# Two halves of a group of transposes sent to TensorE together, and two one-column products made one

## The chip, the core and the metric

The kernel runs on one core of a Trainium2 chip. The metric is the device time of one execution in microseconds; the time before is the median of three runs. The engines are named as in the profile: PE (TensorE, with PEld for its weight loads), DVE (VectorE), ACT (ScalarE), POOL (GpSimd) and SP (SyncE). SP and POOL also issue the transfers (DMA).

## The reference

A delta rule runs over 768 tokens for 4 batches of 8 heads of width 48, and two two-layer networks (384 to 2048 to 384) follow on its 3072 token rows.

```python
k_n = k / (np.linalg.norm(k, axis=-1, keepdims=True) + 1e-06)
for t in range(S):
    kt, vt, bt = (k_n[:, :, t], v[:, :, t], beta[:, :, t, None])
    y[:, :, t] = np.einsum('bhd,bhde->bhe', q[:, :, t], state)
    v_old = np.einsum('bhde,bhd->bhe', state, kt)
    state = state + bt[:, :, :, None] * np.einsum('bhd,bhe->bhde', kt, vt - v_old)
...
h = x @ w_in
g = np.maximum(h, 0.0) + alpha * np.minimum(h, 0.0)
x = g @ w_out
...
h = np.maximum(x @ w_in, 0.0)
return h * h @ w_out
```

## The kernel before

The tokens are cut into 12 chunks of 64, and each chunk into two units, one for each half of the batches and heads (unit u = 2c + s). Three kinds of work run side by side.

**Early work**, unit by unit, ahead of the scan (`early`). `keys` scales the keys, splits them into a high and a low half in 16 bits (`kh`), and spreads them (`ktb`). `transp` (L308) turns both halves: for each half, eight products with an identity go into one PSUM bank (L322), and ACT or DVE copies that bank out three times (`kf`, and `kbd` for each of two heads). `gram` (L339) multiplies them (L344), copies the result out (`gs`, in the trace `r` or `pf`) and stores it to DRAM (`gscr`, L348, from SP's queue). When both chunks of a pair are stored, they are loaded as `prob` (L360), and `inverse` solves 31 columns one after the other on DVE (L386, L387). Its result goes through DRAM (`tscr`, L395) into `diag`.

The banks of early work come from `ebank`: for chunks 0 and 1 four banks in turn (`acc0`, `acc1`, `acc2`, `pe`), from chunk 2 on two banks in turn (`pe`, `acc2`). Each bank has one buffer, so the next user waits until the last copy out of it is done.

**The scan**, chunk by chunk (`steps`, `both`): `b_r` (products of `kbd` with the state `shl`), `b_u0` (with `diag`), `b_go` (with `cross`), `b_u1` (with `diag` again), `b_s` (the new state, `ktb`), `b_p` and `b_y` (the output, products with `sbd` and `ubd`, L131). ACT copies the output out (`t<-pa`), SP stores it (`x1d`, L517) and loads it again as `xf` (L544, L545); ACT and DVE split that into `xh` (L558) and `xl` (L559). Before each chunk, `scales` also finds two powers of two: `ranges` (L257) squares and sums the values and queries into the two columns of `tot` (L265, L266, L268), two products with a matrix of ones sum over the partitions (L271, L272), and a few small DVE operations make the factors `sc`.

**The first network** for each chunk: 16 groups of nine products `h` (L617), an activation on ACT and DVE, a split into `gh` (L629) and `gl` (L630), and nine products `acc` (L649). Layer two follows over pairs of chunks. Before the first chunk, 16 tiles of `w1` are loaded by POOL (L586) and split: ACT copies (`sbd` or `t`, L108), four DVE operations, four products (L597, L598), two casts (L601), two products (L602), two casts (L603).

The order on each engine isn't written by hand. Every step has a time on a list of events (`at`, `run_to`), which sets its priority, and a scheduler places instructions engine by engine from priorities, buffers and modelled times. Each engine then runs its own list strictly in order.

Of the kernel before, what the change touches and what calls it, by code (L numbers as in the profile page):

```python
# [22 lines left out]
CH = 64  # L23
# [6 lines left out]
HD = 2 * D  # L30
# [58 lines left out]
def kernel(ctx: ExitStack, tc: tile.TileContext, qT, ktok, vtok, beta, w1, w2, alpha, cmask, hmask, eye, ident, out):  # L89
# [50 lines left out]
    def ebank(c):  # L140

        return next(two if c > 1 else spare)
# [85 lines left out]
    def scales(c):  # L228
        ss = new(erl, [128, 16], F32, "ss", 2)
        if c:  # L230
            kts[c] = new(erl, [128, 16, D], F32, "ktr")
            G.dma_start(out=kts[c], in_=ktok[c])
        kt = kts[c]
        for v in range(2):
            s2 = bank(128, D, ebank(c))
            A.activation(out=s2, in_=kt[:, 8 * v:8 * v + 8], func=ACTF.Square)
            V.tensor_reduce(out=ss[:, 8 * v:8 * v + 8], in_=s2, axis=AX.X, op=ALU.add)
        n = new(erl, [128, 16], F32, "n", 2)
        r = new(erl, [128, 16], F32, "r", 2)
        A.activation(out=n, in_=ss, func=ACTF.Sqrt)  # L240
        V.tensor_scalar(out=r, in0=n, scalar1=1e-30, scalar2=None, op0=ALU.max)
        V.reciprocal(out=r, in_=r)
        V.tensor_tensor(out=r, in0=ss, in1=r, op=ALU.mult)
        V.tensor_tensor(out=n, in0=n, in1=r, op=ALU.add)
        V.tensor_scalar(out=n, in0=n, scalar1=0.03125, scalar2=6.25e-8, op0=ALU.mult, op1=ALU.add)
        nr[c] = new(erl, [128, 16], F32, "rk", 2)
        V.reciprocal(out=nr[c], in_=n)

        def loads():
            for v in range(2):  # L250
                vs[2 * c + v] = new(stp, [128, NG, D], F32, "vr", 2)
                G.dma_start(out=vs[2 * c + v], in_=vtok[c, :, 8 * v:8 * v + 8])
                qs[2 * c + v] = new(stp, [HD, NG, CH], F32, "qr", 2)
                G.dma_start(out=qs[2 * c + v], in_=qT[2 * c + v])

        def ranges():

            sq = new(erl, [128, 2, 2], F32, "sq", 2)
            for v in range(2):
                for i, t in enumerate((vs[2 * c + v], qs[2 * c + v])):  # L260
                    p = t.shape[0]
                    j = psum.tile([128, 512], F32, tag="pe", name="pe", bufs=PB["pe"])[0:p, 0:NG * t.shape[2]]
                    A.activation(out=j, in_=t.rearrange("p g e -> p (g e)"), func=ACTF.Square, accum_out=sq[0:p, i, v:v + 1])
            tot = new(erl, [128, 2], F32, "tot", 2)
            V.tensor_reduce(out=tot[:, 0:1], in_=sq[:, 0:1], axis=AX.X, op=ALU.add)  # L265
            V.tensor_reduce(out=tot[0:HD, 1:2], in_=sq[0:HD, 1:2], axis=AX.X, op=ALU.add)  # L266
            if c:
                V.tensor_tensor(out=tot[:, 0:1], in0=tot[:, 0:1], in1=cum[0][:, 0:1], op=ALU.add)  # L268
            cum[0] = tot
            ps = psum.tile([128, 512], F32, tag="pe", name="pe", bufs=PB["pe"])  # L270
            nc.tensor.matmul(ps[:, 0:1], lhsT=ones, rhs=tot[:, 0:1], start=True, stop=True)  # L271
            nc.tensor.matmul(ps[:, 1:2], lhsT=ones[0:HD], rhs=tot[0:HD, 1:2], start=True, stop=True)  # L272
            t = new(stp, [128, 8], F32, "sc", 3)
            e = t[:, 0:2].bitcast(U32)
            V.tensor_copy(out=t[:, 0:2], in_=ps[:, 0:2])
            V.tensor_scalar(out=e, in0=e, scalar1=24, scalar2=None, op0=ALU.logical_shift_right)
            V.tensor_scalar(out=e, in0=e, scalar1=-1.0, scalar2=200.0, op0=ALU.mult, op1=ALU.add)
            V.tensor_scalar(out=e, in0=e, scalar1=23, scalar2=None, op0=ALU.logical_shift_left)
            V.reciprocal(out=t[:, 2:4], in_=t[:, 0:2])
            V.tensor_tensor(out=t[:, 3:4], in0=t[:, 2:3], in1=t[:, 3:4], op=ALU.mult)  # L280
            V.tensor_scalar(out=t[:, 4:5], in0=t[:, 2:3], scalar1=0.0625, scalar2=None, op0=ALU.mult)
            V.tensor_scalar(out=t[:, 5:6], in0=t[:, 2:3], scalar1=-0.0625, scalar2=None, op0=ALU.mult)
            V.tensor_scalar(out=t[:, 6:7], in0=t[:, 2:3], scalar1=-0.00390625, scalar2=None, op0=ALU.mult)
            sc[c] = {"v": t[:, 0:1], "q": t[:, 1:2], "y": t[:, 3:4], "s": t[:, 4:5], "r": t[:, 5:6], "g": t[:, 6:7]}

        return loads, ranges
# [3 lines left out]
    def early(u):  # L290
# [16 lines left out]
        def transp():  # L307
# [5 lines left out]
            else:  # L313
                whole = new(erl, [HD, 2, NG, 128], F16, "kbdE") if c else new(stp, [HD, 2, NG, 128], F16, "kbd", 2)
                kbd = [whole[:, i] for i in range(2)]
                kf = new(erl, [HD, 2, NG, CH], F16, "kf") if c else new(stp, [HD, 2, NG, CH], F16, "qh", 2)
            d["kbd"] = kbd
            for i in range(2):
                ps = bank(128, CH, ebank(c))
                for g in range(NG):  # L320
                    w = wide(ktb, i, g)
                    nc.tensor.matmul(ps[0:w.shape[1], g], lhsT=w, rhs=i2, start=True, stop=True)  # L322
                ps = ps[0:HD]
                scaled(kf[:, i], ps)
                for h in range(2):
                    o, k = heads(kbd[i])[:, :, :, h], ps.rearrange("p g (b i) -> p g b i", b=2)
# [495 lines left out]
```

## Time and profile before

| what | us |
|---|---|
| median of three runs | 1141.21 (1141.11 to 1142.35) |
| the profiled execution's own time | 1141.8 |
| its span, first to last instruction | 1140.0 |
| PE, DVE, ACT, POOL busy | 1052.6, 735.1, 729.9, 122.2 |
| mean granted TensorE clock | 0.976 of full speed |

The span has three stages. The opening lasts until the first product `h` of chunk 0 at 153.3 us; the first network and the scan run together until about 755 us; the second network runs alone after that. A busy time says how long an engine worked, not whether anything waited for it; which wait ended last is read from the chain of waits and from the timelines. In a timeline a row gives the start, the time, the engine and line, the tiles written and read, and in brackets the idle time before it with what ended it.

### The profile page before, as it was taken

The page shows a single profiled execution, that of the slowest core. Times are in us where ns is not written, and L with a number is a line of the kernel's source. Part 1 is how long each engine was busy: PE and PEld are TensorE (multiplying, and loading weights), DVE is VectorE, ACT ScalarE, POOL GpSimd, SP SyncE. Part 2 cuts the span into 40 slices and gives each one's busy share as a digit, 9 for nine tenths or more (in the row PEclk, how much of TensorE's full clock was granted, in tenths as well). Part 3 has the DMA queues.
Part 4 walks back from the last instruction along what each step waited for, and adds up shares of the span by engine and source line. Part 5 has one row for each costly group of instructions (what it writes and reads, how often), then busy time and mean ns, then how long its engine had stood idle before and what let it go on. Part 6 is the DMA issues. An engine that isn't in the chain of part 4 may idle for free.

```text
span 1140.0 us, 25239 instructions
## 1 busy us (share of the span) xinstructions
PE 1052.6 (92%) x9952; PEld 934.4 (82%) x9952; DVE 735.1 (64%) x1904; ACT 729.9 (64%) x1583; POOL 122.2 (11%) x214
## 2 busy tenths in 40 slices
PE   2775879899999989998999989999999999999997
PEld 2443579799999988998999989988888888888886
DVE  6969798699889968897996759888312121221211
ACT  7867677867857875885666546577645454554543
POOL 5111111111111111110110001111000000000000
PEclk9887899999999999999999989999999999999999
DMA  9754545744744483555344233343101000010000
GB/s 318 268 138 108 112 134 128 178 127 124 171 109 136 139 176 90 148 146 133 89 110 97 62 112 111 99 137 113 56 1 56 0 28 28 1 56 1 28 1 28
DMA packets 162886, 116.78 MB, mean 102 GB/s; under 512 B 122032, under 2 KB 143536, under 8 KB 162768
## 3 DMA queue, kind: packets, MB, share of 16 engines
q0 software_dynamic: 17472, 73.74, 20.6%
q1 hardware_dynamic: 145296, 41.44, 16.6%
q8 instruction: 78, 1.28, 0.5%
q14 instruction: 40, 0.33, 0.1%
HBM read 75.82 MB, written 39.32 MB: 101 GB/s over the span
## 4 chain that ended last, share of the span: by engine, by line
PE 66%; issue 10%; DMA 7%; ACT 5%; DVE 5%; POOL 1%; SPq 1%; POOLq 0%; DVEq 0%; ACTq 0%
PE h L617 29%; PE acc L649 29%; PE pa L131 4%; PE pa L121 3%; DMA prob<-gscr 2%; DMA gscr<-pf 1%; DMA vr<-in_vtok_dram 1%; DMA xf<-x2d 1%; ACT kbdE L108 1%; SPq L360 1%; ACT r L108 1%; DMA fscr<-kbdE 0%; DVE r L624 0%; DVE gl L630 0%; ACT kf L108 0%
## 5 line engine op out<-in xcount | busy, mean ns | idle before, releaser
L649 PE MATMUL acc<-gh,w 128*128 128x256 f32 (+1 forms) x1728 | 434.2, 323 | 6.6 <-ACT gh L629 5.5
L617 PE MATMUL h<-xh,w 128*128 128x256 f32 (+1 forms) x1728 | 438.4, 324 | 1.2 <-DVE r L624 1.0
L649 PEld LDWEIGHTS acc<-gh,w 128*128 128x128 f32 x1728 | 300.5, 192 | 30.3 <-ACT gh L629 6.1
L630 DVE TENSOR_TENSOR gl<-r,gh 128x256 fp32r<-128x256 f32 (+1 forms) x288 | 145.3, 507 | 277.4 <-ACT gh L629 276.8
L617 PEld LDWEIGHTS h<-xh,w 128*128 128x128 f32 x1728 | 302.8, 191 | 25.1 <-DVE r L624 1.4
L649 PE MATMUL acc<-gl,w 128*128 128x256 f32 (+1 forms) x864 | 276.2, 324 | 2.2 <-DVE gl L630 2.1
L617 PE MATMUL h<-xl,w 128*128 128x256 f32 (+1 forms) x864 | 277.9, 322 | 0.0
L649 PEld LDWEIGHTS acc<-gl,w 128*128 128x128 f32 x864 | 165.8, 192 | 14.8 <-DVE gl L630 3.2
L617 PEld LDWEIGHTS h<-xl,w 128*128 128x128 f32 x864 | 165.7, 192 | 11.3 <-DVE xl L559 0.2
L629 ACT CAST gh<-r 128x256 fp32r<-128x256 f32 (+1 forms) x288 | 136.1, 476 | 49.6 <-DVE r L624 40.0
L626 ACT ACTIVATE r<-h 128x512 f32<-128x512 f32 x96 | 57.1, 596 | 147.9 <-PE h L617 141.0
L108 ACT ACTIVATE r<-h,sgn 128x256 f32<-128x256 f32 x192 | 89.8, 472 | 67.9 <-PE h L617 65.7
L624 DVE SCALAR_TENSOR_TENSOR r<-h,bet,r 128x256 f32<-128x256 f32 x192 | 90.9, 477 | 21.5 <-ACT r L108 20.7
L386 DVE TENSOR_TENSOR col<-prob,inv 128x252 f32<-128x252 f32 (+22 forms) x186 | 63.8, 343 | 1.9
L387 DVE TENSOR_TENSOR inv<-inv,col 128x252 f32<-128x252 f32 (+22 forms) x186 | 63.5, 341 | 1.3
L627 ACT ACTIVATE r<-r 128x512 f32<-128x512 f32 x96 | 60.6, 633 | 2.6
L121 PEld LDWEIGHTS <-kbd 96*128 96x128 f16 x1104 | 37.9, 98 | 11.3 <-issue 8.4
L597 PE MATMUL h<-w,idf 128*128 128x384 f32 x64 | 34.2, 620 | 8.0 <-ACT w L603 7.7
L131 PE MATMUL pa<-ph,ubd 128*128 128x64 f16 (+1 forms) x576 | 39.0, 196 | 0.0
L558 ACT CAST xh<-xf 128x256 fp32r<-128x256 f32 x72 | 25.7, 405 | 17.3 <-DMA xf<-x2d 8.2
L131 PE MATMUL pa<-qh,sbd 96*128 96x64 f16 (+1 forms) x528 | 36.0, 196 | 0.4 <-DVE pf L502 0.4
L559 DVE TENSOR_TENSOR xl<-xf,xh 128x256 fp32r<-128x256 f32 x72 | 26.9, 420 | 13.7 <-ACT xh L558 13.6
(172 smaller groups left out, 1389.2 us busy)
## 6 DMA issues: line engine op xcount, KB each, us to landing
w<-in_w_dram POOLq DMA_DIRECT2D x16, 768.0 KB, 11.9
raw<-in_w_dram POOLq DMA_DIRECT2D x32, 384.0 KB, 3.4
kbd<-fscr POOLq DMA_DIRECT2D x22, 384.0 KB, 4.2
ktb<-kscr POOLq DMA_DIRECT2D x22, 384.0 KB, 3.7
kscr<-ktbE POOLq DMA_DIRECT2D x21, 384.0 KB, 3.5
fscr<-kbdE POOLq DMA_DIRECT2D x21, 384.0 KB, 3.7
vr<-in_vtok_dram POOLq DMA_DIRECT2D x24, 192.0 KB, 3.8
qr<-in_qT_dram POOLq DMA_DIRECT2D x24, 192.0 KB, 3.6
```

The lines of the kernel that those rows point to most:

```text
L108: A.activation(out=out, in_=in_, func=ACTF.Copy if isinstance(scale, float) else ACTF.Identity, scale=scale)
L121: nc.tensor.matmul(ps, lhsT=w[:, i], rhs=x[:, j], start=start and n == 0, stop=stop and n == 2)
L131: nc.tensor.matmul(ps[0:w.shape[1], g], lhsT=w, rhs=x[:, j, g], start=start and n == 0, stop=stop and n == 2)
L386: V.tensor_tensor(out=t, in0=row, in1=x[:, :, 0:m, j:j + 1].to_broadcast([128, 2, m, n]), op=ALU.mult)
L387: i = V.tensor_tensor(out=x[:, :, 0:m, j + 1:], in0=x[:, :, 0:m, j + 1:], in1=t, op=ALU.subtract)
L617: nc.tensor.matmul(ps, lhsT=a[:, sl], rhs=x, start=(n == 0), stop=(n == 8))
L624: V.scalar_tensor_tensor(out=g, in0=ps, scalar=bet[:, j:j + 1], in1=g, op0=ALU.mult, op1=ALU.max)
L626: A.activation(out=g, in_=ps, func=ACTF.Relu)
L627: A.activation(out=g, in_=g, func=ACTF.Square)
L629: A.copy(out=gh, in_=g)
L630: (V if layer or j not in GP else G).tensor_tensor(out=gl, in0=g, in1=gh.bitcast(F32), op=ALU.subtract)
L649: i = nc.tensor.matmul(acc[m], lhsT=a[:, sl], rhs=g, start=(j == 0 and n == 0 and (layer == 1 or m != 1)), stop=(j == NF - 1 and n == 2), ...
```

## The change

The eight transposes of the first half and the eight of the second are issued as one group: both banks are asked for first, all sixteen products are written, and then both banks are copied out. The two products of one column each for the powers of two become one of two columns over all 128 partitions; so that the partitions from 96 on add nothing to the second column, POOL sets it to zero ahead of the sum.

```diff
@@ -262,14 +262,14 @@
                     j = psum.tile([128, 512], F32, tag="pe", name="pe", bufs=PB["pe"])[0:p, 0:NG * t.shape[2]]
                     A.activation(out=j, in_=t.rearrange("p g e -> p (g e)"), func=ACTF.Square, accum_out=sq[0:p, i, v:v + 1])
             tot = new(erl, [128, 2], F32, "tot", 2)
+            G.memset(tot[:, 1:2], 0.0)
             V.tensor_reduce(out=tot[:, 0:1], in_=sq[:, 0:1], axis=AX.X, op=ALU.add)
             V.tensor_reduce(out=tot[0:HD, 1:2], in_=sq[0:HD, 1:2], axis=AX.X, op=ALU.add)
             if c:
                 V.tensor_tensor(out=tot[:, 0:1], in0=tot[:, 0:1], in1=cum[0][:, 0:1], op=ALU.add)
             cum[0] = tot
             ps = psum.tile([128, 512], F32, tag="pe", name="pe", bufs=PB["pe"])
-            nc.tensor.matmul(ps[:, 0:1], lhsT=ones, rhs=tot[:, 0:1], start=True, stop=True)
-            nc.tensor.matmul(ps[:, 1:2], lhsT=ones[0:HD], rhs=tot[0:HD, 1:2], start=True, stop=True)
+            nc.tensor.matmul(ps[:, 0:2], lhsT=ones, rhs=tot, start=True, stop=True)
             t = new(stp, [128, 8], F32, "sc", 3)
             e = t[:, 0:2].bitcast(U32)
             V.tensor_copy(out=t[:, 0:2], in_=ps[:, 0:2])
@@ -315,12 +315,13 @@
                 kbd = [whole[:, i] for i in range(2)]
                 kf = new(erl, [HD, 2, NG, CH], F16, "kf") if c else new(stp, [HD, 2, NG, CH], F16, "qh", 2)
             d["kbd"] = kbd
+            banks = [bank(128, CH, ebank(c)) for i in range(2)]
             for i in range(2):
-                ps = bank(128, CH, ebank(c))
                 for g in range(NG):
                     w = wide(ktb, i, g)
-                    nc.tensor.matmul(ps[0:w.shape[1], g], lhsT=w, rhs=i2, start=True, stop=True)
-                ps = ps[0:HD]
+                    nc.tensor.matmul(banks[i][0:w.shape[1], g], lhsT=w, rhs=i2, start=True, stop=True)
+            for i in range(2):
+                ps = banks[i][0:HD]
                 scaled(kf[:, i], ps)
                 for h in range(2):
                     o, k = heads(kbd[i])[:, :, :, h], ps.rearrange("p g (b i) -> p g b i", b=2)
```

The scheduler places every engine's list anew, so instructions move in many places. Line numbers of the changed kernel are one higher for what stood at L265 to L271 (the one product is L272) and for what stood at L324 and below. Three places follow, with each kernel's own numbers.

ACT in the opening: the copies out of the second half's bank of unit 3 (`w_507` is its `kf` and `kbd`, `acc_508` the bank) until the copy `pf` that unit 3's store to `gscr` takes. Before:

```order
L601 CAST w_1080<-h 128x384 x2
L108 ACTIVATE w_507<-acc_508 96x512
L108 ACTIVATE w_507<-acc_508,hm 96x16x32 x2
L603 CAST w_1080<-h 128x384 x2
L108 ACTIVATE sbd<-w_1340 128x384
L108 ACTIVATE sbd<-w_1340,sge 128x384
L108 ACTIVATE pf<-pe 64x8x32 x2
L236 ACTIVATE acc_614<-ktr 128x384
```

Now:

```order
L604 CAST w_1117<-h 128x384
L108 ACTIVATE sbd<-w_1340 128x384
L604 CAST w_1117<-h 128x384
L108 ACTIVATE sbd<-w_1340,sge 128x384
L108 ACTIVATE w_507<-acc_508 96x512
L108 ACTIVATE w_507<-acc_508,hm 96x16x32 x2
L108 ACTIVATE t<-w_1365 128x384
L108 ACTIVATE t<-w_1365,sge 128x384
L236 ACTIVATE acc_614<-ktr 128x384
L602 CAST w_1165<-h 128x384 x2
L108 ACTIVATE pf<-pe 64x8x32 x2
```

The casts for `w_1117` and the first two for `w_1165`, the copies to `t` and L236 now stand ahead of `pf` (two more casts for `w_1117`, L602, stand just above this piece); they stood behind it.

POOL's queue around the store of unit 3's transposed keys (`fscr_148`) and the last two loads of `w1`. Before:

```order
L254 DMA qr<-in_qT_dram 96x512
L335 DMA fscr_148<-w_507 96x1024
L586 DMA w_1517<-in_w_dram 128x768
L461 DMA kbd<-fscr_147 96x2048
L586 DMA w_1495<-in_w_dram 128x768
```

Now:

```order
L254 DMA qr<-in_qT_dram 96x512
L587 DMA w_1517<-in_w_dram 128x768
L336 DMA fscr_148<-w_507 96x1024
L462 DMA kbd<-fscr_147 96x2048
L587 DMA w_1495<-in_w_dram 128x768
```

The load of `w_1517` now stands ahead of the second store to `fscr_148`.

ACT at the start of chunk 4 of the first network (`rhl_87` is the first right-hand side of the scan's next chunk, `xh_6104` to `xh_6108` the input of chunk 4). Before, from the row behind the last `t<-pa` of chunk 4 on:

```order
L108 ACTIVATE r_6055<-h,sgn 128x256
L108 ACTIVATE rhl_87<-vr,sc 64x384
L108 ACTIVATE r_6088<-h,sgn 128x256
L629 CAST gh<-r_6055 128x256
L108 ACTIVATE kh<-ktr 128x384
L629 CAST gh<-r_6088 128x256
L108 ACTIVATE r_6162<-h,sgn 128x256
L108 ACTIVATE rhl_87<-vr,sc 64x384
L108 ACTIVATE r_6215<-h,sgn 128x256
L629 CAST gh<-r_6162 128x256
L108 ACTIVATE kh<-ktr 128x384
L558 CAST xh_6104<-xf 128x256
```

Now, from the last `t<-pa` of chunk 4 on:

```order
L108 ACTIVATE t<-pa,sc 96x4x64 x2
L108 ACTIVATE r_6215<-h,sgn 128x256
L108 ACTIVATE rhl_87<-vr,sc 64x384
L108 ACTIVATE r_6311<-h,sgn 128x256
L630 CAST gh<-r_6215 128x256
L108 ACTIVATE kh<-ktr 128x384
L559 CAST xh_6104<-xf 128x256
L559 CAST xh_6106<-xf 128x256
L559 CAST xh_6108<-xf 128x256
L630 CAST gh<-r_6311 128x256
L108 ACTIVATE rhl_87<-vr,sc 64x384
```

Between the last copy of the output and the first `xh` there stood eleven rows before, and there stand five now; the second `rhl_87` moved from ahead of `xh` to behind it.

## Rows read from the trace of the kernel before

**Rows 1.** The page, part 1: busy time, share of the span, instructions of each engine.
```profile
PE 1052.6 (92%) x9952; PEld 934.4 (82%) x9952; DVE 735.1 (64%) x1904; ACT 729.9 (64%) x1583; POOL 122.2 (11%) x214
```

**Rows 2.** Windows of 20 us: stretch, busy PE, PEld, DVE, ACT, POOL, PEclk, DMA share, GB/s.
```profile
400.00:420.00 20.00, 17.00 (x201) 16.43 (x201) 12.65 (x30) 15.41 (x37) 2.56 (x4) 1.00 0.84 173
420.00:440.00 20.00, 17.68 (x234) 16.76 (x234) 15.72 (x50) 10.27 (x28) 2.91 (x5) 0.93 0.48 111
```

**Rows 3.** The chain of waits, opening: start, us, what.
```profile
53.91 10.56 DMA gscr<-pf
...
66.32 3.17 DMA prob<-gscr
```

**Rows 4.** Timeline of ACT in the opening: start, us, line, operation, idle before.
```profile
51.15 0.86 ACT L603 CAST w<-h 128x384 fp32r<-128x384 f32 x2
...
53.80 0.48 ACT L236 ACTIVATE acc<-ktr 128x384 f32<-128x384 f32 x1
54.30 0.56 ACT L108 ACTIVATE t<-w 128x384 f32<-128x384 f32 x1
...
54.76 0.63 ACT L108 ACTIVATE t<-w,sge 128x384 f32<-128x384 f32 x1
```

**Rows 5.** Timeline of PE in the opening: two rounds of w1.
```profile
58.82 0.94 PE L597 MATMUL h<-w,idf 128*128 128x384 f32 x2 [0.19 <-ACT w L603]
...
63.38 0.94 PE L597 MATMUL h<-w,idf 128*128 128x384 f32 x2 [0.19 <-ACT w L603]
```

**Rows 6.** Windows of 2 us in the opening, columns as in rows 2.
```profile
58.00:60.00 2.00, 1.81 (x6) 0.92 (x6) 0.52 (x1) 1.82 (x5) 0.00 (x0) 1.00 1.10 305
```

**Rows 7.** POOL timeline, chain of waits, DMA issues by line (KB, us to landing).
```profile
52.12 0.55 POOL L586 DMA_DIRECT2D w<-in_w_dram  x1
...
180.10 5.28 DMA gscr<-pf
...
gscr<-pf SPq DMA_DIRECT2D x21, 128.0 KB, 3.1
```

**Rows 8.** Timeline of DVE at the start of the first inversion.
```profile
70.64 0.56 DVE L237 TENSOR_REDUCE ss<-pe 128x8 f32<-128x384 f32 x1
...
71.50 0.17 DVE L241 TENSOR_SCALAR r<-n 128x16 f32<-128x16 f32 x1
...
72.96 0.25 DVE L247 RECIPROCAL rk<-n 128x16 f32<-128x16 f32 x1
```

**Rows 9.** Chunk 4: timelines of PE, SP, ACT; DMA issues; source line L559.
```profile
346.87 0.30 PE L131 MATMUL pa<-ph,ubd 128*96 128x64 f16 x3
...
342.71 6.38 SPq L517 DMA_DIRECT2D x1d<-t  x2
...
351.72 0.91 SPq L545 DMA_DIRECT2D xf<-x1d  x1
...
xf<-x1d SPq DMA_DIRECT2D x12, 96.0 KB, 3.5
...
358.06 0.77 ACT L558 CAST xh<-xf 128x256 fp32r<-128x256 f32 x2 [0.62 <-PE h L617]
...
L559 DVE TENSOR_TENSOR xl<-xf,xh x72: 406/419/427, 151.3 to 1063.6; 128x256 fp32r<-128x256 f32 x72
```

**Rows 10.** The chain of waits in the first layer: rates of PE.
```profile
477.78 2.16 PE h L617 x18
...
339.42 2.20 PE pa L131 x72
```

**Rows 11.** Timelines of PE, DVE and POOL at the powers of chunk 7.
```profile
435.95 0.36 PE L272 MATMUL pe<-tot,ones 96*128 96x1 f32 x2
436.17 0.42 PE L131 MATMUL pa<-uh,ktb 128*128 128x48 f16 x8
...
435.44 0.15 DVE L268 TENSOR_TENSOR tot<-tot 128x1 f32<-128x1 f32 x1
...
436.89 0.54 POOL L467 DMA_DIRECT2D ktb<-kscr  x1 [8.92 <-PE pa L131]
```

## The prediction

> **What bounds the kernel now.** I read the busy shares first, then the chain of waits from its start, then windows and timelines where the changed order of the engines touches that chain. PE is busy for 1052.6 of 1140.0 us [rows 1], so a microsecond gained elsewhere counts only where PE waits. There are three stages. In the opening, up to the first product `h` at 153.3, the end is set by the first inversion on DVE and what follows it; the chain runs back from it through a load of `prob` to the store of `pf` to `gscr`, which started at 53.91 and took 10.56 us [rows 3]. That is unit 3's store, the last of the pair. In the second stage PE works its list in order with little room: of the two stretches of 20 us shown it was busy for 17.00 and 17.68, and idle for 3.0 and 2.3 [rows 2], the largest idle times I found there. The third stage is products of the second network alone, and the change touches nothing in it.
>
> The sum is made against the profiled execution's own 1141.8, which lies 0.6 above the median of 1141.21; that 0.6 is taken off at the end. A change of 0.2%, 2.3 us, is about what a measurement of this kernel can tell from none.
>
> **The group of transposes itself: 0.** The order of PE shows that the eight products of one half and of the other already stood next to each other in most even units; in most odd units other products still stand between them after the change, since the second bank (`pe`) is still held by an earlier user. The number of products and copies is the same. What the edit does is reorder every engine's list, and this is costed below, place by place.
>
> **The powers of two: -2.2.** Each of the 12 pairs becomes one product. At chunk 7 the pair stood at 435.95 and the next product at 436.17, so a pair takes 0.22 [rows 11], as two records. Two of the twelve lie in the opening, where PE is not what ends last; for the ten others I take the whole of a pair's second product at the 0.22 of the pair, so 10 x 0.22 = 2.2. Bounds: half of it, since only one of the two products goes, 1.1; and the record's own 0.36 each, 3.6. I take the middle because the product that goes also waits for its own operand. The Trainium skill, page "TensorE: Matmul & The Clock Gate", section "Wait — 56ns, not 53.3ns?", says that products follow one another by no less than about 25 ns, however few columns they have; an estimate by that floor alone would be 10 x 0.025 = 0.25 instead of 2.2. Here the row of 0.22 for two such records speaks against so low a price.
>
> **The added zero on POOL: 0.** Its 12 small operations stand behind the loads of the chunk's values on POOL, ahead of a load of `ktb`. `tot` has two buffers, so the zero waits for the sum two uses back, and with it POOL's queue. At chunk 7 the sum ran at 435.44, and the load of `ktb` was issued at 436.89, after 8.92 of waiting for PE [rows 11]: it had to wait longer than the zero would have. If the cover is gone, a load comes late by what the sum is late, and with it the state `b_s`; this is in the upper end.
>
> **The opening: 0, between -4.9 and +5.0.** Four things move.
> 1. The copy `pf`, which starts the store, now has more ahead of it on ACT: six casts of `w1`, two of which took 0.86 [rows 4], so 0.43 each and 2.6 in all; the two copies to `t`, 0.56 and 0.63; and L236, 0.48 [rows 4]. Together 4.3, the lower bound of its delay. Those casts need products of PE and subtractions of DVE, so `pf` can wait for rounds of `w1`: from 58.82 to 63.38 one round is 4.56 [rows 5]. At most one and a half rounds and the copies, 6.8 + 1.7 = 8.5.
> 2. The store itself took 10.56 while a load of `w1`, issued by POOL at 52.12 [rows 7], was under way, and the DMA engines were full: share 1.10 and 305 GB/s from 58 to 60 [rows 6]. Now that load is issued earlier, ahead of unit 3's store of its transposed keys, and the store finds less traffic. Another store of the same kind took 5.28 on the chain, and the median of 21 is 3.1 [rows 7]: -5.3 to -7.5. So it lands between 3.2 earlier (4.3 - 7.5) and 3.2 later (8.5 - 5.3).
> 3. A sum of squares and six small operations of DVE, for chunk 2, stood after 70.64 among the first columns of the inversion, and now stand ahead of it: 0.56 and six between 0.17 and 0.25 [rows 8], -1.7.
> 4. The high part of the inverse is cast by ACT, and the cast now stands behind two `pf`, a `go` and a `kf`: 0 to +1.8, with 0.45 for each by the casts of [rows 4].
>
> The ends are -3.2 - 1.7 + 0 = -4.9 and +3.2 + 0 + 1.8 = +5.0, taking no gain from the third at the upper end because DVE may then be waiting anyway. Neither is nearer to a row, so I take 0.
>
> **Starts of chunks 4 and 6: +4.2.** Between the last product of the scan's output and the first `h` of the next chunk the scan's result goes out and back through DRAM and is split. At chunk 4 that last product was at 346.87 and took 0.30, ended 347.17. The load `xf` was issued at 351.72 and lands 3.5 later, at 355.2; the split takes 0.39 for the first `xh` (two took 0.77) and 0.42 for `xl` [rows 9]. So 8.1 + 0.8 = 8.9 us of other products must stand in that place. The row of the first `xh` shows that ACT was then waiting for PE, not for the load [rows 9]: covered. In PE's order I counted those products: before chunk 4, 86 large (256 columns) and 88 small; now 41 and 48. At 2.16/18 = 0.12 and 2.20/72 = 0.031 [rows 10] that is 13.0 before and 6.4 now. Before chunk 6 it was 90 and 120, 14.5; now 48 and 48, 7.2. The other chunks keep over 8.9. PE thus waits 8.9 - 6.4 = 2.5 and 8.9 - 7.2 = 1.7, together 4.2. Bounds: 0, where that idle time only takes the place of a later one, and 6.0 where the issue's 0.91 [rows 9] comes on top of the 3.5 at each.
>
> **The second right-hand side: +1.0.** `rhl`'s second half now stands on ACT behind three `xh`, which wait for the load; the first diagonal product of the next chunk waits for it. Two `xh` took 0.77 [rows 9], so up to 1.0 at each of two chunks, or nothing where PE is still occupied; 0 to 2.0, taken as +1.0.
>
> **Sum:** 0 - 2.2 + 0 + 0 + 4.2 + 1.0 = +3.0: 1144.8 for an execution like the profiled one, less 0.6 is **1144.2**. The opening must not come out by more than 0.7 shorter for this to show as slower by over 0.2%.
>
> **The rivals.**
> *A shorter opening (faster).* If the store finds the queues free, it lands after 3.1 instead of 10.56, and if `pf` is late by only the 4.3 of ACT's own work, the inversion starts 3.2 earlier and loses 1.7 of small work: -4.9. With -2.2 and the waits of +4.2 as above, and no `rhl` wait, -2.9: 1138.3. If the waits at chunks 4 and 6 are swallowed too, -7.1: 1134.1. The point from which it decides is the landing of the store: before 64.47 (53.91 + 10.56) it gains, after it loses. For it speaks that the store's 10.56 is an exception among 21, against it that six casts depend on PE's rounds.
> *The waits are swallowed (same).* The idle time of 400 to 440, 3.0 + 2.3 = 5.3 us [rows 2], comes right behind chunk 4's start. Where PE waits there for DVE and ACT, which go on working while PE is held at 359, a delay of 2.5 at chunk 4 and 0.5 of `rhl` is given back: 3.0 - 3.0 = 0, 1141.2. Against it speaks that part of that idle time lies with the granted clock at 0.93 and DVE busy for 15.72 of 20 [rows 2].
> *The change does not do what it says.* If the transposes stay apart, only the new order counts; I already cost the group at 0, so this moves nothing.
> On the slower side of the forecast lies a wait of POOL's queue for the zero, which would make a load late at each chunk; it is the upper end.
>
> **How the numbers follow.** The forecast has 0.45, A 0.30, "swallowed" 0.25. I hold the forecast likeliest because its counts of products come straight from the order and the path it must cover is measured, while the opening has terms of both signs. The lowest sum is -4.9 - 3.6 + 0 + 0 = -8.5, 1132.7; the highest +5.0 - 1.1 + 6.0 + 2.0 = +11.9, 1153.1. All bounds at once are unlikely, so the range goes from 1134.0 (A with its waits swallowed) to 1151.0 (the opening and the starts of chunks 4 and 6 at their upper ends: 5.0 - 2.2 + 6.0 + 1.0 = +9.8). As both signs hold much of the chance: the forecast's own range is 1143.5 to 1151.0. Faster by over 0.2% (below 1138.9) is A, 0.30; within it 0.25; slower (above 1143.5) 0.45.
>
> **What would show it.** Right: the first `h` of chunk 0 near 153.3; waits of PE for `xh` or `xl` of some 2.5 and 1.7 at the starts of chunks 4 and 6, and none there at chunk 5; 12 products fewer at the powers; the load of `ktb` released by PE still, not by the zero. A is right if unit 3's store lands well before 64.5 and the first `h` comes before 150. "Swallowed" is right if those two waits are there and the idle time of 400 to 440 is smaller by as much. The forecast is wrong if PE meets `xf` in time, or if a wait that isn't in this list costs more than 2 us.

## The result and the profile after

The changed kernel took 1157.87 us, the median of four runs (1155.34 to 1161.83), beside 1141.78 for the kernel before in the same comparison: a ratio of 1.0119 with a 95% interval of 1.0088 to 1.0150. It is **slower by 1.2%** in the ratio; the medians are 16.1 us apart, where 3.0 were forecast, and the time lies above the stated range. The profiled execution is the 1161.83; its span is 1159.8, and its mean granted clock is 0.958, against 0.976 before.

First the busy line, which answers to [rows 1]; then windows with the columns of [rows 2], of 3 us at the starts of chunks 4 and 6, and the two stretches that answer to those of [rows 2]:

```profile
PE 1066.8 (92%) x9928; PEld 944.5 (81%) x9928; DVE 737.5 (64%) x1904; ACT 730.3 (63%) x1583; POOL 123.6 (11%) x226
```

```profile
368.00:371.00 3.00, 1.24 (x11) 1.03 (x9) 2.00 (x5) 0.41 (x2) 0.00 (x0) 1.00 0.43 141
371.00:374.00 3.00, 2.96 (x16) 2.86 (x17) 2.91 (x8) 1.53 (x4) 0.00 (x0) 0.63 0.00 0
...
479.00:482.00 3.00, 3.00 (x20) 3.00 (x19) 2.21 (x6) 1.36 (x3) 0.67 (x2) 0.67 0.33 131
400.00:420.00 20.00, 20.00 (x323) 19.70 (x321) 19.69 (x67) 15.06 (x33) 3.56 (x7) 1.00 0.50 149
420.00:440.00 20.00, 16.54 (x192) 15.42 (x191) 11.54 (x27) 16.14 (x40) 2.52 (x4) 1.00 0.79 165
```

PE has 24 records fewer than in [rows 1] and is busy for 14.2 us more, while its idle time, span less busy, grew by only 5.6 (from 87.4 to 93.0). So most of the loss is not waiting, it is PE working slowly: behind each of the waits at chunks 4 and 6 a window of 3 us has a mean granted clock of 0.63 or 0.67, where it was 1.00 before, that is, 1.2 in place of 2.4 GHz for two thirds of the window or more. The window from 371 to 374 holds 16 products, where 25 would fit at the 0.12 of [rows 10].

The waits themselves, from PE's timeline, with the rows of SP and ACT that the one at chunk 4 follows from (they answer to [rows 9]):

```profile
161.09 0.79 PE L618 MATMUL h<-xh,w 128*128 128x256 f32 x2 [3.08 <-ACT xh L559]
...
242.11 0.58 PE L618 MATMUL h<-xh,w 128*128 128x256 f32 x1 [2.09 <-DVE r L625]
...
371.05 0.39 PE L618 MATMUL h<-xh,w 128*128 128x256 f32 x1 [1.81 <-ACT xh L559]
...
475.46 0.39 PE L618 MATMUL h<-xh,w 128*128 128x256 f32 x1 [1.83 <-ACT xh L559]
...
530.66 0.58 PE L650 MATMUL acc<-gl,w 128*128 128x256 f32 x1 [3.14 <-DVE gl L631]
...
367.42 0.41 SPq L546 DMA_DIRECT2D xf<-x1d  x1
...
370.59 1.02 ACT L559 CAST xh<-xf 128x256 fp32r<-128x256 f32 x3 [3.09 <-DMA xf<-x1d]
```

At chunk 4, ACT waited 3.09 for the load of `xf`, issued at 367.42, and PE waited 1.81 for `xh`; at chunk 6, 1.83. These are the two waits that the prediction names. The others (3.08 at chunk 0, 2.09 for `r` and 3.14 for `gl`) it does not name.

The opening, in the timelines of ACT, SP and DVE (they answer to [rows 3], [rows 4] and [rows 7]):

```profile
69.37 0.45 ACT L108 ACTIVATE go<-pe 64x256 f16<-64x256 f32 x1 [0.70 <-DMA oscr<-go]
...
60.67 0.38 SPq L349 DMA_DIRECT2D gscr<-pf  x1
64.05 0.46 SPq L353 DMA_DIRECT2D oscr<-go  x1
64.61 1.20 SPq L361 DMA_DIRECT2D prob<-gscr  x2
70.33 0.46 SPq L353 DMA_DIRECT2D oscr<-go  x1
70.84 1.24 SPq L361 DMA_DIRECT2D prob<-gscr  x2
...
73.82 0.69 DVE L381 SCALAR_TENSOR_TENSOR prob<-prob,bt 128x512 f32<-128x512 f32 x1 [0.75 <-DMA prob<-gscr]
```

Unit 3's store is issued at 60.67, 6.8 later than the 53.91 of [rows 3]. It lands in under 4, since the load that needs it is issued at 64.61. But two of the four loads of `prob` stand in SP's queue behind a second store of `go` (70.33), and that one waits for ACT's `go` at 69.37, which itself waits until the first store of `go` has emptied its buffer (0.70, after ACT had waited 3.61 for PE's products of `w1`). The last piece of `prob` reaches DVE at 73.82; before, the load had landed at 69.5 (66.32 + 3.17 [rows 3]).

At the powers of two of chunk 7, first the row of the kernel before that stands ahead of those in [rows 11], then the changed kernel's:

```profile
435.74 0.35 PE L271 MATMUL pe<-tot,ones 128*128 128x1 f32 x2 [1.19 <-DVE tot L266]
```

```profile
453.22 0.35 PE L272 MATMUL pe<-tot,ones 128*128 128x2 f32 x2 [0.16 <-DVE tot L267]
453.44 0.72 PE L131 MATMUL pa<-uh,ktb 128*128 128x48 f16 x20
```

The wide product has two records, as each narrow one had, and takes the same 0.22 to the next product. POOL's zero (L265) did wait for an older sum, 19.5 us in five places; whether that cost anything is the third experiment's question.

### The profile page after: what moved, and what is told of

Its sections match the earlier page's. It is cut to its first block, busy times and chain, and to the rows that moved or that the text cites. A ratio compares the mean times of both kernels' runs of the same rounds, so it can differ in the third digit from the quotient of the medians.

```text
span 1159.8 us, 25227 instructions
## 1 busy us (share of the span) xinstructions
PE 1066.8 (92%) x9928; PEld 944.5 (81%) x9928; DVE 737.5 (64%) x1904; ACT 730.3 (63%) x1583; POOL 123.6 (11%) x226
## 3 DMA queue, kind: packets, MB, share of 16 engines
q0 software_dynamic: 17472, 73.74, 20.5%
## 4 chain that ended last, share of the span: by engine, by line
PE 65%; DMA 11%; issue 9%; DVE 7%; ACT 5%; SPq 2%; POOL 1%; ACTq 0%; POOLq 0%; DVEq 0%
PE h L618 28%; PE acc L650 28%; PE pa L131 4%; PE pa L121 3%; DMA kscr<-ktbE 2%; DMA x1d<-t 1%; DMA prob<-gscr 1%; DMA xf<-x1d 1%; DMA vr<-in_vtok_dram 1%; PE h L598 1%; PE h L599 1%; DVE r L625 1%; DMA raw<-in_w_dram 1%; DVE col L387 1%; DVE inv L388 1%
## 5 line engine op out<-in xcount | busy, mean ns | idle before, releaser
L618 PE MATMUL h<-xh,w 128*128 128x256 f32 (+1 forms) x1728 | 444.1, 327 | 11.4 <-ACT xh L559 8.4
L650 PE MATMUL acc<-gh,w 128*128 128x256 f32 (+1 forms) x1728 | 437.4, 325 | 6.8 <-ACT gh L630 6.5
L618 PEld LDWEIGHTS h<-xh,w 128*128 128x128 f32 x1728 | 307.7, 195 | 35.9 <-ACT xh L559 9.3
L650 PEld LDWEIGHTS acc<-gh,w 128*128 128x128 f32 x1728 | 304.4, 194 | 30.9 <-ACT gh L630 7.8
L618 PE MATMUL h<-xl,w 128*128 128x256 f32 (+1 forms) x864 | 281.2, 325 | 0.0
L618 PEld LDWEIGHTS h<-xl,w 128*128 128x128 f32 x864 | 168.7, 195 | 11.5 <-DVE r L625 0.2
L598 PE MATMUL h<-w,idf 128*128 128x384 f32 x64 | 36.9, 666 | 12.5 <-ACT w L604 9.9
L559 ACT CAST xh<-xf 128x256 fp32r<-128x256 f32 x72 | 25.1, 406 | 27.7 <-DMA xf<-x1d 12.2
L560 DVE TENSOR_TENSOR xl<-xf,xh 128x256 fp32r<-128x256 f32 x72 | 26.8, 419 | 20.7 <-ACT xh L559 20.7
```

The source lines that it names most:

```text
L618: nc.tensor.matmul(ps, lhsT=a[:, sl], rhs=x, start=(n == 0), stop=(n == 8))
L650: i = nc.tensor.matmul(acc[m], lhsT=a[:, sl], rhs=g, start=(j == 0 and n == 0 and (layer == 1 or m != 1)), stop=(j == NF - 1 and n == 2), ...
```

## The experiments

The new lists of all engines left three candidates: the operations of the change themselves, the order, or the chance that a fresh execution draws. The theory was that **the order is all**: a late store in the opening, waits of PE at new places, and the clock's fall behind each. The rivals are written into the expectations. Each run is compared with the kernel before on its own chip: 1145.05 there for the first four, 1145.69 for the next four, 1144.53 for the last three.

**1. Only the grouping.** The second hunk of the diff alone.

> Only the grouping of the transposes, the two products of the powers as before. Its order differs from the kernel before in 12 rows of PE in the opening and on no other engine. Theory 'order': the time is set by the order of the engines, which the grouping alone leaves in place: 1141 us, within 2 us of before. Rival 'banks': two banks held together delay the copies or the next user of a bank: 1148 to 1158, with the loss in the opening and at the odd units.

Measured: 1143.58, ratio 0.9995 (0.9967 to 1.0023). The grouping alone neither costs nor gains. It moves 12 rows on one engine; 'banks' falls.

**2. The wide product in the old order.**

```diff
...
-            tot = new(erl, [128, 2], F32, "tot", 2)
+            tot = tots[c % 2]
...
-            nc.tensor.matmul(ps[:, 0:1], lhsT=ones, rhs=tot[:, 0:1], start=True, stop=True)
-            nc.tensor.matmul(ps[:, 1:2], lhsT=ones[0:HD], rhs=tot[0:HD, 1:2], start=True, stop=True)
+            nc.tensor.matmul(ps[:, 0:2], lhsT=ones, rhs=tot, start=True, stop=True)
+            nc.tensor.matmul(ps[:, 2:3], lhsT=ones[0:HD], rhs=tot[0:HD, 1:2], start=True, stop=True)
```

> The two-column product of the change in the order of before: the two buffers of tot are zeroed once at the start, the product of two columns over 128 partitions is there, and a second product of one column goes into a column that nobody reads, so that PE has as many instructions as before (43 rows of PE differ, nearly none elsewhere). Theory 'order': 1141 us, within 2.5 us of before. Rival 'operation': the product over 128 partitions of the second column, or what its result waits for, costs by itself: 1146 or more.

Measured: 1142.92, ratio 0.9993 (0.9971 to 1.0016). The wide product costs nothing either. What slows the kernel is neither the grouping nor the wide product.

**3. The change without POOL's zeros.** The whole change with `tots` as above, zeroed once, and the one product.

> The whole change, but with the two buffers of tot zeroed once at the start in place of POOL's zero in each chunk. PE's order is that of the change row for row, ACT differs in 4 rows, SP in 2. Theory 'order': as slow as the change, 1155 to 1162, first h of chunk 0 near 161, waits of PE for xh at the starts of chunks 4 and 6 of 1.8 each. Rival 'POOL': the zero holds POOL's queue and makes loads late: faster than the change by over 5 us, 1150 or less.

```profile
366.15 0.56 PE L620 MATMUL h<-xh,w 128*128 128x256 f32 x2 [1.86 <-ACT xh L561]
...
470.11 0.39 PE L620 MATMUL h<-xh,w 128*128 128x256 f32 x1 [2.35 <-ACT xh L561]
```

Measured: 1153.68, ratio 1.0080 (1.0046 to 1.0114). Still slow, with the same two waits (1.86 and 2.35). It is a little under the expected 1155, and its interval overlaps that of the change (1.0070 to 1.0121 in run 5), so a small part of the zeros isn't excluded, but it is not what makes the change slow.

**4. Only the powers.** The first hunk alone.

> Only the one product with POOL's zero, the transposes as before. In the opening its order is that of the change (the store of unit 3 behind the casts of one and a half more rounds of w1, one go store between the last loads of prob), but before chunks 4 and 6 stand 18.3 us of products each, against 6.4 and 7.2 in the change. Theory 'order': the opening's 7.8 is lost, first h of chunk 0 near 161, no wait for xh at chunks 4 and 6: 1146 to 1151. Rival 'clock alone': the time follows the number of stretches at the lower clock, which any new order draws anew: no relation to the opening, 1140 to 1160.

```profile
211.45 0.58 PE L617 MATMUL h<-xh,w 128*128 128x256 f32 x1 [5.25 <-DVE r L624]
...
340.55 0.35 PE L272 MATMUL pe<-tot,ones 128*128 128x2 f32 x2 [1.18 <-POOL tot L265]
```

Measured: 1152.02, ratio 1.0079 (1.0040 to 1.0117): one microsecond above what was expected, and inside the wide range of 'clock alone', which this run does not exclude. The first `h` came at 158.4, not near 161. No wait for `xh` at chunks 4 and 6, as the count of products said, but a wait of 5.25 for `r` at 211.45 that no count had shown. One wait of PE was released by POOL's zero (1.18 at 340.55). Merging two tiny products, with POOL's zero, is enough to redraw the order, and the grouping, which does nothing by itself, redraws it again when it comes on top.

**5. The change again,** for a second profile beside the next three.

> The changed kernel itself, on the chip of the three kernels behind it, so that they can be compared with it. Theory 'order': 1.0 to 1.4% above before, the same waits of PE as in its first profile (for xh at the starts of chunks 4 and 6, 1.8 each, and before chunks 0 and 1), since they are in its order; the granted clock differs from run to run and moves its time by some microseconds. Rival 'chance': the waits are elsewhere in this profile.

```profile
370.34 0.50 PE L618 MATMUL h<-xh,w 128*128 128x256 f32 x2 [2.09 <-ACT xh L559]
```

Measured: 1157.68, ratio 1.0095 (1.0070 to 1.0121), just under the expected 1.0 to 1.4%, with the same waits in the same places (2.09 at chunk 4, 1.78 at chunk 6). 'Chance' falls for the waits. For the clock it does not fall: behind the 2.09 it was at half for 3.41 us, behind the 1.78 it stayed at 1.00.

**6. The opening put back.** One constraint on PE's order.

```diff
...
-            nc.tensor.matmul(ps[i], lhsT=idf, rhs=f[:, DM * i:DM * i + DM], start=True, stop=False)
+            with behind(("T", 3) if j == 99 else ("G", 3) if j == 3 else None):
+                nc.tensor.matmul(ps[i], lhsT=idf, rhs=f[:, DM * i:DM * i + DM], start=True, stop=False)
```

> The change with one constraint: the fourth round of w1 is queued on PE behind the products of unit 3's gram. The copy pf and the store of unit 3 come ahead of the casts for two rounds of w1 again, and SP's loads of prob stand together again. All later orders are drawn anew: before chunk 4 stand 5.4 us of products, before chunk 6 22. Theory 'order': the store is issued 4 to 8 us earlier (near 55), the first h of chunk 0 comes 2 to 7 us earlier than in the change; a wait of some 3 us for xh stays at chunk 4 and the one at chunk 6 is gone; 3 to 9 us below the change. Rival 'clock alone': no relation, the change's time within 3 us.

```profile
56.21 0.37 SPq L356 DMA_DIRECT2D gscr<-pf  x1
...
363.14 0.50 PE L626 MATMUL h<-xh,w 128*128 128x256 f32 x2 [2.94 <-ACT xh L566]
```

Measured: 1150.86, ratio 1.0050 (1.0025 to 1.0075), 6.8 below the change in the medians, 0.45% or 5.2 in the ratios. The store is issued at 56.21, the first `h` comes at 154.6 (161.9 in run 5), the wait at chunk 4 is there with 2.94 and that at chunk 6 is gone. As expected, though everything behind the opening was redrawn too, so the gain is not the opening's alone.

**7. The starts of chunks 4 and 6 put back.** One constraint, the opening left late.

```diff
+                done[c] = mm3w(ps, d["ubd"], d["p"], g, c == 0, True)
...
-        emit_h(layer, t, j)
+        with tc.issue_after(done[t + 1]) if layer == 0 and t + 1 in (4, 6) and j == 11 else nullcontext():
+            emit_h(layer, t, j)
```

> The change with one constraint: the products h of group 11 of chunks 3 and 5 are queued on PE behind the last product of the next chunk's output. 10.1 and 10.0 us of products then stand before chunks 4 and 6, in place of 6.4 and 7.2; up to chunk 3 the order is the change's row for row. Theory 'waits with their clock': the waits of 1.8 for xh at chunks 4 and 6 are gone, and with each a stretch of 3.4 us at half the clock, which costs 1.7: 2 x (1.8 + 1.7) = 7 us below the change. Rival 'idle alone': 3.6 us below it. Rival 'moved': the scan is late anyway, PE waits for it elsewhere, within 2 us of the change.

The windows around the first `h` of chunk 4 (367.9) and of chunk 6 (469.6):

```profile
364.00:368.00 4.00, 4.00 (x54) 3.91 (x52) 3.97 (x11) 2.64 (x8) 0.06 (x1) 1.00 0.45 120
368.00:372.00 4.00, 4.00 (x65) 3.96 (x64) 3.95 (x11) 3.95 (x9) 1.05 (x2) 1.00 0.36 117
...
466.00:470.00 4.00, 4.00 (x53) 3.96 (x53) 3.48 (x9) 1.63 (x6) 0.00 (x0) 1.00 0.26 78
470.00:474.00 4.00, 3.95 (x54) 3.75 (x52) 4.00 (x12) 3.54 (x9) 1.11 (x2) 1.00 0.41 127
```

A later wait of the same run, and the window behind it:

```profile
527.44 0.39 PE L651 MATMUL acc<-gl,w 128*128 128x256 f32 x1 [3.18 <-DVE gl L632]
...
527.00:531.00 4.00, 3.56 (x47) 3.52 (x48) 3.08 (x9) 2.46 (x7) 0.00 (x0) 1.00 0.16 40
```

Measured: 1149.76, ratio 1.0040 (1.0012 to 1.0067), 7.9 below the change in the medians, 0.55% or 6.3 in the ratios. PE is full across both starts and the clock stays at 1.00. That is nearer to the 7 of 'waits with their clock' than to the 3.6 of 'idle alone', but the gap between the two, 0.3%, is smaller than one interval is wide; run 10 was made to tell them apart better. The wait of 3.18 for `gl` at 527.44 was followed by no fall of the clock.

**8. Both put back.** The constraint of run 6, and that of run 7 for chunk 4 alone with group 10.

> The change with both: the fourth round of w1 behind unit 3's gram, and h of group 10 of chunk 3 behind the output of chunk 4. The opening is as in the run before this one; 12 us of products and more stand before every chunk from 2 on, 9.6 before chunk 1. Theory 'order': opening and starts are repaired and the change's own operations cost nothing: within 0.5% of before, 1139 to 1148 where before is at 1143. Rival: something else of the change costs, 1151 or more.

```profile
208.77 1.25 PE L121 MATMUL pa<-rhl,diag 128*128 128x48 f16 x24 [2.78 <-DMA diag<-tscr]
...
419.47 0.76 PE L121 MATMUL pa<-rhl,diag 128*128 128x48 f16 x24 [3.54 <-DMA diag<-tscr]
...
678.09 0.58 PE L659 MATMUL acc<-gh,w 128*128 128x256 f32 x1 [4.04 <-ACT xf L668]
```

Measured: 1152.40, ratio 1.0047 (1.0019 to 1.0076): the median is 4 above the expected range and lies where the rival, that something else of the change costs, was expected (1151 or more). The two repairs don't add up. Runs 1 to 3 found no operation of the change that costs as much; what the profile shows is that the order was drawn a fifth time (up to 337 us it is that of run 6) and brought waits of its own: 2.78 and 3.54 for `diag`, 4.04 near 678. The count of products before each chunk, all that I had controlled, says nothing of these. That they are the whole excess is not shown.

**9. What a wait costs.** The kernel before with eight waits of known length in its last stage.

```diff
+    def stall(n, m):
...
+        for i in range(n):
+            V.tensor_copy(out=zs[(i + 1) % 2], in_=zs[i % 2])
+        V.tensor_copy(out=cell, in_=zs[n % 2][:, 0:1])
+        return nc.tensor.matmul(ps[:, 0:1], lhsT=ones, rhs=cell, start=True, stop=True).ins
...
```

> The kernel before with eight waits put into the second network, where nothing else holds PE (its order is otherwise the same): PE makes one product, DVE copies its result 3, 6, 10 or 16 times in PSUM one after the other, and PE's next product needs the last copy. Each length is there twice, once with PE empty meanwhile and once with 6, 9, 14 or 21 spare products of 128 columns that need nothing. The empty waits should be some 1.3, 2, 3 and 4.5 us. Theory 'waits with their clock': behind the empty waits of 2 us and more stands a stretch of 3.4 us at half the clock, which costs 1.7 on top of the wait; behind the filled ones of the same length none. Rival 'idle alone': the clock stays at 1.00 behind all, and the second network grows by the waits alone. Rival 'chance': half-clock stretches come with no relation to the waits.

PE's timeline at six of the eight closing products, and the windows at or behind them:

```profile
819.67 0.38 PE L676 MATMUL pe<-cell,ones 128*128 128x1 f32 x2 [2.11 <-DVE cell L675]
...
890.72 0.56 PE L676 MATMUL pe<-cell,ones 128*128 128x1 f32 x2 [2.74 <-DVE cell L675]
...
929.71 0.38 PE L676 MATMUL pe<-cell,ones 128*128 128x1 f32 x2 [0.53 <-DVE cell L675]
...
967.19 0.56 PE L676 MATMUL pe<-cell,ones 128*128 128x1 f32 x2 [4.08 <-DVE cell L675]
...
1002.82 3.29 PE L672 MATMUL pe<-idf,ones 128*128 128x128 f32 x28
...
1046.33 0.56 PE L676 MATMUL pe<-cell,ones 128*128 128x1 f32 x2 [6.08 <-DVE cell L675]
...
1087.72 0.38 PE L676 MATMUL pe<-cell,ones 128*128 128x1 f32 x2 [1.18 <-DVE cell L675]
```

```profile
820.00:824.00 4.00, 4.00 (x19) 3.31 (x19) 0.00 (x0) 1.67 (x3) 0.00 (x0) 1.00 0.00 0
...
891.00:895.00 4.00, 4.00 (x11) 3.23 (x11) 0.00 (x0) 0.00 (x0) 0.00 (x0) 0.50 0.00 0
...
934.00:938.00 4.00, 4.00 (x19) 3.31 (x18) 0.69 (x1) 1.76 (x4) 0.00 (x0) 1.00 0.00 0
...
966.00:970.00 4.00, 2.81 (x8) 2.36 (x9) 0.94 (x4) 0.00 (x0) 0.00 (x0) 0.50 0.00 0
...
1045.00:1049.00 4.00, 2.67 (x7) 2.25 (x8) 1.05 (x4) 0.00 (x0) 0.00 (x0) 0.50 0.00 0
...
1092.00:1096.00 4.00, 4.00 (x19) 3.32 (x18) 0.69 (x1) 1.77 (x4) 0.00 (x0) 1.00 0.01 4
```

The empty waits of 2.74, 4.08 and 6.08 are each followed by PEclk 0.50: in the 4 us from 891, PE makes 11 records where it makes 19 at 1.00. Behind the empty wait of 2.11 the clock stays at 1.00, and so it does behind all four that spare products filled, though DVE's chains were as long there. So the clock follows what PE does in a wait, not the wait for DVE. Three misses: the empty wait of 2.11 had no stretch behind it, against the theory; the empty waits came out longer than meant (2.11 to 6.08 in place of 1.3 to 4.5), and the clock behind them was at half for nothing or for 6.8 us, never for the expected 3.4. Each stretch began before its wait ended (0.2, 1.6 and 2.2 us), so these three waits cost themselves and another 3.3, 2.6 and 2.3: half of the part in which PE worked. The second network grew from 394.9 to 437.4 us: 17.7 of idle time, 10.2 from the clock (half of 3 x 6.83), 11.7 of spare products (100 records at 0.117, as in 3.29 for 28), and 3.5 for the 16 opening and closing ones at 0.22 come to 43.1, or 41.1 if the clock is counted only where PE worked. The run took 1.0350 (1.0293 to 1.0406) of before, as it should. The Trainium skill, page "TensorE: Matmul & The Clock Gate", section "HAM oscillation — how this bites in real kernels", describes a loop in which PE waits for a load in each step and starts the next at the lower clock each time. Here each wait stands alone and is for DVE, and this trace agrees for the empty waits of 2.74, 4.08 and 6.08.

**10. One wait taken out of the kernel before.** In its profile ACT held `gh` behind `xh` of the second network's first step, which waited 5.02 for its load:

```profile
671.79 1.02 ACT L558 CAST xh<-xf 128x256 fp32r<-128x256 f32 x3 [5.02 <-DMA xf<-x2d]
...
673.17 0.58 PE L649 MATMUL acc<-gh,w 128*128 128x256 f32 x1 [3.57 <-ACT gh L629]
...
669.00:673.00 4.00, 0.60 (x6) 0.40 (x4) 0.77 (x3) 1.21 (x4) 0.00 (x0) 0.97 0.48 179
673.00:677.00 4.00, 3.83 (x16) 3.57 (x17) 3.73 (x11) 2.72 (x8) 0.00 (x0) 0.50 0.50 161
677.00:681.00 4.00, 4.00 (x26) 4.00 (x25) 2.50 (x7) 0.92 (x2) 0.00 (x0) 0.67 0.31 73
```

```diff
-                A.copy(out=xh[:, cols], in_=t[:, m])
+                with tc.issue_after(cast[0, 11, 4]) if n == NCH else nullcontext():
+                    A.copy(out=xh[:, cols], in_=t[:, m])
...
-        A.copy(out=gh, in_=g)
+        cast[layer, t, j] = A.copy(out=gh, in_=g).ins
```

> The kernel before with one constraint on ACT: the high parts xh of the first step of the second network are cast behind the fifth gh of the last chunk of the first. Before, they stood on ACT ahead of gh of chunk 10 and held it until their load landed, so that PE waited 3.57 for gh at 673.17, and the clock was at half for 6.83 behind it. Up to there the order is that of before row for row. Theory 'waits with their clock': 3.6 + 3.4 = 7 us faster than before, 0.994; rival 'idle alone': 3.6 us faster, 0.997; rival 'moved': gh or xh is late in another place, no change.

The first two of these stretches in the run:

```profile
669.00:673.00 4.00, 4.00 (x36) 4.00 (x35) 1.39 (x3) 2.60 (x7) 0.18 (x1) 1.00 0.92 274
673.00:677.00 4.00, 4.00 (x36) 4.00 (x35) 3.86 (x11) 2.51 (x7) 0.00 (x0) 1.00 0.67 237
```

Measured: 1135.96, ratio **0.9933** (0.9907 to 0.9959). 0.67% is 7.7 us, with an interval from 4.7 to 10.6: the 7.0 of 'waits with their clock' lies in it, the 3.6 of 'idle alone' (0.997) outside. The 6.83 at half clock belong to the first profile alone: in runs 1, 2, 9 and 11 the same wait was 3.5 to 3.9 long and 3.41 at half clock followed it, a price of 5.2 to 5.6, which lies in the interval too. In the one profile of this run the first network is 3.8 shorter than the mean of the old order (table below) and the second 0.8, so the 7.7 rests on the medians. This run beats both kernels.

**11. The kernel before again.**

> The kernel before itself, for a second profile of it on the chip of these runs. Theory 'order': the same waits of PE as in its first profile (for shl near 203, go near 406, diag near 520, gh near 673), the first h of chunk 0 between 153 and 158, since it was 153.3 in the first profile and 157.5 and 156.2 in the two runs with its order. Rival 'chance': the opening is as long as with the change's order, 158 to 162.

```profile
73.71 1.03 DVE L380 SCALAR_TENSOR_TENSOR prob<-prob,bt 128x512 f32<-128x512 f32 x2
```

Measured: 1142.85, ratio 0.9989 (0.9959 to 1.0019). The waits stand where they stood, except that the wait for `shl` is shorter and split. The first `h` came at 158.4, just outside what was expected and as late as in runs 4 (158.4) and 7 (157.8), whose openings have the change's late store. The last piece of `prob` came to DVE at 73.71, as late as in the change, without a second store of `go` ahead of its load. The opening differs by several us between executions of one order, so single profiles can't price it.

## Why the prediction was wrong

Reading the first network of all profiles the same way shows where the time went. Idle is the sum of the gaps between PE's products from the first `h` of chunk 0 to the first `h` of the second network, "half" the time in it at which 0.50 of the clock was granted, and the rest is the length less idle and less half of "half" (all us):

| kernel | first h | length | idle | half | rest |
|---|---|---|---|---|---|
| before | 153.3 | 585.9 | 23.5 | 20.5 | 552.1 |
| 1, grouping alone | 157.5 | 582.9 | 23.8 | 13.7 | 552.3 |
| 2, wide product, old order | 156.2 | 585.9 | 24.5 | 17.1 | 552.9 |
| 9, waits in the second network | 152.1 | 584.5 | 25.3 | 13.7 | 552.4 |
| 11, before again | 158.4 | 586.3 | 24.7 | 20.4 | 551.4 |
| the change | 161.1 | 598.8 | 27.0 | 46.9 | 548.4 |
| 5, the change again | 161.9 | 595.3 | 29.2 | 31.7 | 550.3 |
| 3, without POOL's zeros | 159.1 | 593.0 | 28.6 | 29.9 | 549.5 |
| 4, powers alone | 158.4 | 590.8 | 27.9 | 23.4 | 551.2 |
| 6, opening back | 154.6 | 591.1 | 26.9 | 32.9 | 547.8 |
| 7, starts back | 157.8 | 590.2 | 24.7 | 30.1 | 550.5 |
| 8, both back | 155.8 | 589.7 | 26.8 | 29.3 | 548.3 |
| 10, one wait gone | 155.1 | 581.3 | 20.5 | 13.7 | 554.0 |

Between the five profiles with the order of before and the three with that of the change, the means give: opening 155.5 to 160.7, **+5.2**; idle 24.4 to 28.3, **+3.9**; half 17.1 to 36.2, which costs half of 19.1, **+9.6**; rest 552.2 to 549.4, **-2.8**. The sum is +15.9, and the second network is 0.8 shorter; the medians say +16.1 and +12.0. PE was idle in a part of the time at half clock, up to 3.1 us in these profiles, and this part is counted twice; without it the clock's term is +8.8 and the rest -2.1.

- **The clock: the step that failed.** The prediction priced each wait of PE at its length: "PE thus waits 8.9 - 6.4 = 2.5 and 8.9 - 7.2 = 1.7, together 4.2." The waits were there, 1.81 and 1.83. But PE's clock fell behind such waits (for 3.41 us behind each of the two in the first profile), and the clock is the largest term, +8.8 to +9.6, for which the sum has no line. Only a part of it belongs to these two waits: 6.8 of the 46.9 us at half clock in the first profile, 3.4 of 31.7 in run 5. With their clock added the sum would have been some +6.4. The rest lies at places that the prediction did not count. The profile had it: PEclk 0.93 in [rows 2] was read as a reason why an idle time wouldn't shrink, not as part of the price of a wait. Nor were those two stretches the ones with the most idle time: from 200 to 220 PE was idle for 3.8 us with the clock at 0.91, from 660 to 680 for 3.6 us at 0.83.
- **Waits that were not counted.** Only one path, from the output of the scan to `xh`, was counted in the new order. The waits for `xh` at chunk 0, for `r` and for `gl` are new as well (the first of them belongs to the opening), each of more than the 2 us that the prediction had named as a sign of being wrong; some of before (2.16 for `shl`, 1.91 for `go`) are gone, and in place of 3.57 for `gh` there are 2.25 and 2.77; the net idle time, +3.9, comes near the forecast +5.2 (4.2 and 1.0 for `rhl`), but by other items: no wait over 0.75 was released by `rhl` in the change.
- **The opening: 0 forecast, +5.2 in the means.** Two of its terms were right: the store was issued 6.8 later (4.3 to 8.5 forecast) and took under 4 in place of 10.56 (5.3 to 7.5 less forecast), and so landed when it had landed before. That was rival A's decisive point, and it came out even. What was lost was lost behind it, in SP's queue, which was not read for this stage: in the first profile a second store of `go` between the loads of `prob` put the last piece of `prob` back from 69.5 to 73.8, 4.3 us. But runs 2 and 11, in the old order, have it at 73.7 too. In the means of the same five and three profiles it comes at 71.7 and 74.6, so 3.0 of the 5.2 arise up to there; the other 2.2 arise behind it, and their cause stays open.
- **The group: 0, right** (run 1). **POOL's zero: 0**; run 3 doesn't exclude a few us, run 4 shows one wait of 1.18.
- **The powers: -2.2 forecast, -2 to -3 measured,** by a misreading. The 0.22 of [rows 11] is the price of the second product alone, with its two records; the first stands ahead of it (435.74), and the pair took 0.43. So the 0.22 per product was right, and the bound of half of it, 1.1, was not. The rest is 549.4 in the mean of the seven kernels with one product and 552.5 in the six with two, -3.1, or -2.0 without what is counted twice; single profiles differ by more than that. The prediction's estimate by the floor in the Trainium skill, page "TensorE: Matmul & The Clock Gate", section "Wait — 56ns, not 53.3ns?", 0.25 in all, is too small here, where one such product took 0.21 to 0.22.
- **'Swallowed'** was wrong: the idle time of 400 to 440 went from 5.3 to 3.5, but new waits took its place. The two windows don't hold the same work any more: ACT cast the first `xh` of chunk 4 at 358.06 before [rows 9] and at 370.59 now.

The forecast had the right sign and two of its waits; it was a fifth of the size. That its idle time and its powers came out near the measured ones was in part luck. The range failed at the upper end for the same reason, since its worst case held no clock either.

What stays open: why the new lists bring more waits of 2 to 3 us than the old one. All five new orders measured (the change and runs 4, 6, 7 and 8) have more idle time, and more time at half clock, than the mean of the old one; these five are not independent draws, since run 7 has the change's order up to about 350 us and run 8 that of run 6 up to 337, and no run tells whether the old order is a rare one or the new ones share a cause.

## What to carry to other kernels

Where a scheduler places the instructions, an edit that saves two microseconds is also a new draw of the order, and the order was worth 12 to 16 here (the medians of two comparisons); read every engine's queue on the path, SP's too, and keep the old order by a constraint if the edit is to be judged by itself. Price a wait of PE by its length and by the clock that may fall behind it (some 3.6 of waiting were worth 7.7, between 4.7 and 10.6, in run 10), and look for the one wait that a single constraint takes away, rather than for products to save.

## What the runs showed of the hardware that was not expected

- In run 9 the clock followed PE's emptiness: with spare products in the wait it stayed at 1.00, behind an empty 2.74 it was at 0.50. But the length of one wait doesn't decide: 2.11 in run 9, 1.78 in run 5 and 3.18 in run 7 left the clock at 1.00, 1.81 and 1.83 in the change did not, and in the kernel before 3.41 us at half clock from 229.05 had no wait of over 1 us in the 8 us ahead of them (0.98 at 228.44).
- One program differs by more than a percent between executions: the kernel before took 1133.79 (mean clock 0.980) to 1149.33 (0.971) in 23 runs on the second chip. The 0.2% that the prediction took as measurable holds for medians of many runs at best; three runs on the first chip had looked far quieter, and a fourth there took 1152.54.
